# A new order of all operations in a convolution, layer norm and feed-forward kernel, and a scaling in two one-column operations

## The chip, the cores and the metric

The kernel runs on one core of one Trainium2 chip. The metric is the device time of one execution in microseconds (us). A core has a matrix engine (TensorE, PE in the profile, its weight loads PEld), VectorE (DVE), ScalarE (ACT), GpSimd (POOL) and SyncE (SP), which here only issues transfers. Each works through a queue of its own in order and waits for the others by semaphores.

## What is computed

The input `x` has 8 sequences of 4224 tokens with 192 features. Every token first becomes a weighted sum of itself and its six predecessors (a dynamic convolution: 7 weights for each token and each of 8 heads, by a softmax), then goes through a layer norm with gain `g_ln`, a two-layer feed-forward network with 768 hidden features, and a residual addition:

```python
w = np.exp(weight_gen - max); w = w / (np.sum(w, axis=-1, keepdims=True) + 1e-09)
out = np.einsum('bshk,bskhg->bshg', w, x_unf)            # x_unf: the token and 6 predecessors
mu, var = mean and variance of each token's 192 features
xn = (x - mu) / np.sqrt(var + 1e-06) * g_ln
ch = np.maximum(xn @ w_ch1, 0.0) @ w_ch2
return (x + ch).astype(np.float32)
```

(In the last three lines `x` is the convolution's result.) The weights of the network come as 64-bit floats.

## The kernel before

**Tiling.** The 33,792 tokens lie over 128 partitions, 264 columns each. Columns go in parts of 4, 8 or 12 (`PARTS`), the convolution in chunks of up to 6 columns, the network in 66 groups of 4 columns. `x` is kept in a ring of 36 columns.

**Convolution (`conv`).** SyncE loads `x` and the softmax weights `w`. `softmax` makes the exponent's argument with maxima `mx` and sums `sm` on VectorE (L461, L477), operand steps on GpSimd (L463, L481) and exponentials and a logarithm on ScalarE. `conv` multiplies on VectorE (L530): product 0 goes into the buffer `y`, six more, two at a time, into three buffers `pr`. From the fourth chunk on four of the six are added to `y` by GpSimd (L533, steps `a0` to `a3`); the other two are first added to a neighbour in `pr` by a DMA that GpSimd issues and that adds at its destination (L536, steps `d0` and `d1`; here called a sum by DMA).

**Layer norm (`norm`).** ScalarE sums and squares each token (L604, L609), VectorE refines the reciprocal root, ScalarE scales to `xh` (L653). The first two groups are transposed by TensorE (L676), the rest split into a high half (ScalarE, `hl`, L722) and a remainder (GpSimd, `hl`, L724) and transposed by a DMA from SyncE (L728, step `turn`) to `xT`.

**Network.** TensorE multiplies a group in three units (L746, step `unit`) into two PSUM tiles `ph`; of each unit ScalarE writes `hh` (L762) and VectorE the remainder `hlo` (L764), which frees the tile. The second layer runs in two halves a group (L798, steps `p0` and `p1`), the last group in four whole outputs (L827). VectorE adds the result to `y` (L850) and SyncE stores it (L858, step `u`).

**Weights (`weights`).** At the start the 64-bit weights are converted (`from_double`, L916 to L933). `w_scale` sums their squares with TensorE (L944, into `po`) and takes the reciprocal of a power of two from it in four one-column steps on VectorE (L948 to L952); after them it multiplies the gain `g`, two columns, by that number into `gi` (L954). ScalarE scales the weights with `gi`; TensorE makes the low halves (L994, for the second matrix the corrections L1040 and L1041), ScalarE copies them (L999, L1045).

**What sets the order.** Every operation is given to `Plan.op` with a name, and takes the next number from that name's row in the table `PLACE` (L38 on). `Plan.order` sorts all operations by these numbers; each engine's queue is that order, cut to its own operations. It also hands out buffers in this order, each operation to the one that was last used earliest. Two kinds of transfers are kept apart: a transpose waits until the last sum by DMA ahead of it has landed, and the other way round.

```python
o.key, o.place = want, PLACE[want[0]][i]
...
out = sorted(self.ops, key=lambda o: o.place)
...
if o.kind in last:
    o.behind, last[o.kind] = last["turn" if o.kind == "add" else "add"], o
```

Of the kernel before, what the change touches and what calls it, by code (L numbers as in the profile page):

```python
# [38 lines left out]
    'wload': (0, 1, 13, 40, 43, 97, 228, 492, 500, 297, 610, 771, 667, 953, 949, 1143, 1284, 1244, 1047, 1445,  # L39
        1553, 1626, 1733,),  # L40
    'load': (2, 3, 5, 7, 9, 23, 48, 51, 50, 138, 140, 136, 277, 226, 273, 288, 291, 417, 336, 488, 613, 564,
        665, 740, 634, 732, 856, 840, 873, 945, 927, 1011, 1069, 1247, 1287, 1311, 1210, 1378, 1371, 1411, 1492,
        1653, 1517, 1623, 1777, 1703, 1852, 1924, 1915, 1959, 2014, 1954,),
    'w_load': (27, 15, 21,),
    'w_gain': (30, 46, 38,),
    'w_load2': (32,),
    'w_as': (71,),
    'w_av': (80, 83, 86,),
    'w_an': (89,),
    'w_cs': (57,),  # L50
# [12 lines left out]
    'w_d2': (168,),
    'w_h2': (175, 173, 193,),
    'w_l2': (187, 181, 196,),
    'w_lc2': (192, 188, 203,),
    'max': (4, 11, 52, 111, 114, 323, 268, 540, 596, 592, 705, 826, 893, 1097, 1129, 1175, 1347, 1345, 1483,
        1606, 1622, 1723, 1911,),
    'sub': (6, 16, 60, 115, 238, 347, 462, 581, 606, 702, 776, 902, 999, 1102, 1136, 1265, 1369, 1421, 1543,
        1630, 1768, 1814, 2007,),  # L70
    'exp': (8, 22, 66, 147, 263, 364, 491, 601, 636, 744, 803, 931, 1037, 1113, 1144, 1277, 1387, 1449, 1563,
        1638, 1792, 1849, 2041,),
    'sum': (10, 26, 93, 180, 285, 390, 496, 605, 645, 756, 818, 946, 1044, 1138, 1150, 1280, 1436, 1451, 1609,
        1654, 1807, 1890, 2063,),
    'log': (12, 29, 100, 184, 293, 407, 501, 609, 663, 772, 841, 968, 1058, 1147, 1216, 1285, 1450, 1490, 1679,
        1750, 1847, 1894, 2075,),
    'less': (14, 31, 109, 185, 316, 410, 514, 612, 689, 787, 883, 980, 1063, 1166, 1295, 1359, 1456, 1546, 1690,
        1781, 1861, 1935, 2103,),
    'expw': (17, 20, 35, 45, 119, 137, 155, 202, 210, 274, 331, 337, 378, 429, 450, 521, 530, 629, 643, 718,
        731, 811, 830, 904, 936, 1000, 1031, 1116, 1109, 1204, 1215, 1312, 1351, 1415, 1391, 1516, 1500, 1601,  # L80
        1627, 1710, 1726, 1811, 1805, 1871, 1968, 1964, 2039, 2132, 2122, 2206,),
    'keep': (18, 39, 63,),
# [16 lines left out]
    'copy': (54, 73, 101,),  # L99
    'sums': (58, 75, 104, 107, 152, 169, 204, 217, 239, 237, 259, 279, 329, 319, 348, 344, 393, 413, 424, 426,  # L100
# [7 lines left out]
    'squares': (69, 79, 124, 110, 163, 171, 212, 224, 242, 286, 267, 282, 339, 332, 350, 355, 409, 415, 435,  # L108
# [7 lines left out]
    'rstd': (81, 134, 178, 233, 289, 359, 441, 512, 594, 699, 808, 901, 1007, 1110, 1213, 1304, 1426, 1519,  # L116
# [167 lines left out]
def kernel(  # L284
# [673 lines left out]
    def weights():  # L958
        F2 = F // 2
        wac, w2r = Buf("hlo"), Buf("hlo")  # L960
        wa, wc = (wac, "a"), (wac, "c")
        s1, s2, r1, r2, g, gi = (W[k] for k in ("s1", "s2", "r1", "r2", "g", "gi"))
# [69 lines left out]
        z2 = [Buf("ph"), Buf("ph")]  # L1032
# [77 lines left out]
```

## Time and profile before

| | us |
|---|---|
| three timed runs | 860.5, 862.37, 863.0 |
| their median | 862.37 |
| the profiled execution | 856.82 |
| its span, from the first to the last instruction | 855.0 |
| busy in it: TensorE | 820.9 |
| VectorE | 740.9 |
| ScalarE | 691.1 |
| GpSimd | 701.9 |

The profile is of one execution. A timeline row gives the start in us from the span's start, how long it took, the engine, the line of the kernel, the operation, what it writes and reads, and how many equal ones it merges; in brackets stands how long the engine had been idle and what released it. "issue" as the releaser means that the engine waited for nothing that the profile shows. A `q` behind an engine (SPq) marks its sequencer, which issues transfers. "To landing" is the time from a transfer's issue until all of it has arrived.

### The profile page before, as it was taken

The numbers are of one execution on the slowest core, as the hardware profiler recorded it, in microseconds if no ns is written. First come the engines' busy times: TensorE is split into PE (matmuls) and PEld (weight loads), VectorE is DVE, ScalarE is ACT, GpSimd is POOL, SyncE is SP. The second block draws the span as 40 slices with busy tenths as digits, with TensorE's granted clock in tenths as the row PEclk, the third lists the DMA queues.
The fourth block names the chain that finished last, engine by engine and source line by source line (L and its number), as shares of the span: only waits on it lengthen the run. The fifth ranks groups of instructions, "written<-read, shape, count | busy, mean of one in ns | idle before, by whom it ended". The sixth has DMA issues, their size and how long they took to land.

```text
span 855.0 us, 37401 instructions
## 1 busy us (share of the span) xinstructions
PE 820.9 (96%) x16696; PEld 804.3 (94%) x16696; DVE 740.9 (87%) x692; ACT 691.1 (81%) x1804; POOL 701.9 (82%) x402
## 2 busy tenths in 40 slices
PE   6669999999999999999999999999999999999997
PEld 5349999999999999999999999999999999999997
DVE  7999999999999999999999899889898797655442
ACT  5889988889988889989987888798878987786431
POOL 4799999999999999999999889997898678572200
PEclk9789999999999999999999999999999999999999
DMA  8689999889998999978989599897786853555332
GB/s 238 152 169 181 211 168 186 187 185 214 175 212 153 195 214 175 197 166 193 209 163 228 133 169 196 148 192 165 160 201 150 164 127 80 110 114 86 67 105 57
DMA packets 133888, 140.89 MB, mean 165 GB/s; under 512 B 104294, under 2 KB 106222, under 8 KB 133726
## 3 DMA queue, kind: packets, MB, share of 16 engines
q1 hardware_dynamic: 120190, 88.16, 47.8%
q0 software_dynamic: 13536, 50.34, 30.6%
q8 instruction: 130, 2.13, 1.0%
q14 instruction: 32, 0.26, 0.1%
HBM read 36.43 MB, written 25.95 MB: 73 GB/s over the span
## 4 chain that ended last, share of the span: by engine, by line
PE 88%; DVE 6%; ACT 3%; issue 2%; DMA 1%; SPq 0%; DVEq 0%; ACTq 0%
PE po L798 44%; PE ph L746 43%; DVE pr L530 3%; DVE hlo L764 1%; PE ph L827 1%; DMA x<-in_x_dram 1%; ACT xh L653 1%; DVE y L530 1%; ACT junk L604 0%; ACT junk L609 0%; PE ph L1040 0%; DVE mx L461 0%; DVE hlo L930 0%; ACT hh L762 0%; SPq L423 0%
## 5 line engine op out<-in xcount | busy, mean ns | idle before, releaser
L533 POOL TENSOR_TENSOR y<-y,pr 128x1152 f32<-128x1152 f32 (+1 forms) x188 | 482.4, 2583 | 25.6 <-DVE y L530 8.9
L746 PE MATMUL ph<-xT,c_w 64*128 64x256 f16 x7128 | 416.5, 269 | 3.0 <-DVE hlo L764 2.2
L746 PEld LDWEIGHTS <-c_w 64*128 64x128 f16 x7128 | 386.9, 94 | 9.4 <-issue 7.1
L798 PE MATMUL po<-c_w2l,hh 64*128 64x192 f16 x3120 | 392.1, 243 | 2.5 <-issue 2.5
L798 PE MATMUL po<-c_w2h,hlo 64*128 64x192 f16 x3120 | 392.0, 243 | 1.7 <-issue 1.7
L798 PE MATMUL po<-c_w2h,hh 64*128 64x192 f16 x3120 | 391.8, 243 | 0.1
L798 PEld LDWEIGHTS <-hh 64*128 64x128 f16 x6240 | 340.2, 94 | 4.1 <-issue 3.9
L530 DVE TENSOR_TENSOR pr<-x,wn 128x2304 f32<-128x2304 f32 (+2 forms) x147 | 333.2, 2276 | 4.3 <-POOL y L533 2.7
L764 DVE SCALAR_TENSOR_TENSOR hlo<-ph,hh 128x1024 f16<-128x1024 f32 x198 | 238.7, 1217 | 81.4 <-ACT hh L762 81.0
L762 ACT ACTIVATE hh<-ph 128x1024 f16<-128x1024 f32 x198 | 200.2, 1014 | 88.8 <-PE ph L746 81.9
L798 PEld LDWEIGHTS <-hlo 64*128 64x128 f16 x3120 | 213.6, 94 | 2.3 <-issue 2.3
L724 POOL TENSOR_TENSOR hl<-xh,hl 128x768 f16<-128x768 f32 x64 | 115.7, 1857 | 41.3 <-ACT hl L722 41.2
L653 ACT ACTIVATE xh<-y,s 128x192 f32<-128x192 f32 x264 | 126.4, 538 | 11.5 <-DVE s L641 7.2
L609 ACT ACTIVATE junk<-y,s 128x192 f32<-128x192 f32 x264 | 120.0, 455 | 9.5 <-PE po L798 3.2
L536 POOL DMA_DIRECT2D pr<-pr x94 | 93.3, 1083 | 38.1 <-DVE pr L530 14.3
L604 ACT ACTIVATE junk<-y 128x192 f32<-128x192 f32 x264 | 95.4, 361 | 12.3 <-PE po L798 5.2
L850 DVE SCALAR_TENSOR_TENSOR y<-po,c_fs,y 128x768 f32<-128x768 f32 (+1 forms) x83 | 68.2, 835 | 7.4 <-PE po L798 7.3
L530 DVE TENSOR_TENSOR y<-x,wn 128x1152 f32<-128x1152 f32 (+2 forms) x50 | 59.9, 1199 | 0.0
L722 ACT ACTIVATE hl<-xh 128x768 f16<-128x768 f32 x64 | 53.6, 838 | 2.6 <-PE po L798 1.7
L604 ACT ACTIVATION_READ_ACCUMULATOR junk<-y 128x1 f32 x264 | 50.0, 189 | 0.0
L609 ACT ACTIVATION_READ_ACCUMULATOR junk<-y,s 128x1 f32 x264 | 49.8, 189 | 0.0
L463 POOL TENSOR_TENSOR e<-w,mx 128x672 f32<-128x672 f32 (+2 forms) x23 | 34.6, 1503 | 5.0 <-issue 2.8
(79 smaller groups left out, 302.5 us busy)
## 6 DMA issues: line engine op xcount, KB each, us to landing
pr<-pr POOLq DMA_DIRECT2D x68, 576.0 KB, 6.8
x<-in_x_dram SPq DMA_DIRECT2D x34, 576.0 KB, 6.5
out_dram<-y SPq DMA_DIRECT2D x34, 576.0 KB, 5.5
pr<-pr POOLq DMA_DIRECT2D x26, 384.0 KB, 5.1
w<-in_weight_gen_dram SPq DMA_DIRECT2D x21, 336.0 KB, 6.2
x<-in_x_dram SPq DMA_DIRECT2D x14, 384.0 KB, 6.1
out_dram<-y SPq DMA_DIRECT2D x13, 384.0 KB, 3.7
x<-in_moe_w_ch_dram SPq DMA_DIRECT2D x1, 1152.0 KB, 12.2
```

The costliest lines, as they stand in the source:

```text
L530: E.tensor_tensor(out=ov, in0=xv, in1=wv, op=ALU.mult)
L533: Q.tensor_tensor(out=flat(0), in0=flat(0), in1=flat(k), op=ALU.add)
L536: return Q.dma_start(flat(to), flat(k), accum_op=ALU.add, max_dma_last_dim=CHUNK * D * 4)
L604: A.activation(junk, at(y)[:, j, :], AF.Identity, scale=-SQ / D, accum_out=at(s4)[:, 3, t : t + 1])
L609: A.activation(junk, at(y)[:, j, :], AF.Square, scale=SQ, bias=at(s4)[:, 3, t : t + 1], accum_out=at(s4)[:, 0, t : t + 1])
L653: A.activation(paired(xh, t), at(y)[:, i, :].rearrange("p (c q) -> p c q", q=P // 2), AF.Identity, bias=at(s4)[:, 3, g + t : g + t + 1], s ...
L724: lambda xh=xh, hl=hl: Q.tensor_tensor(out=halves(hl, True), in0=pairs(xh), in1=halves(hl, False), op=ALU.subtract),
L746: T_.matmul(ph[:, r, v * 2 * P : (v + 1) * 2 * P], W["w1"][rows, WB[r][c], w, f : f + P], xv[rows, a, c, :, :], start=(v == 0 and k == 0), ...
L762: lambda: A.activation(at(hh)[:, us, :], at(ph), AF.Relu), [ph], [(hh, u)])
L764: lambda: V.scalar_tensor_tensor(out=at(hlo)[:, us, :], in0=at(ph), scalar=0.0, in1=at(hh)[:, us, :], op0=ALU.max, op1=ALU.subtract),
L798: made.append(T_.matmul(at(po)[:, z, e * D : (e + 1) * D], token(b, 2 * z + e, j)[rows], W[w][rows, j, :], start=(ph == 0 and e == 0 and k ...
L850: V.scalar_tensor_tensor(out=ysl, in0=at(po)[:, zs[0] : zs[-1] + 1, : 2 * D], scalar=W["fs"][:, 0:1], in1=ysl, op0=ALU.mult, op1=ALU.add)
```

## The change

The table `PLACE` gets other numbers in nearly every row, found by a search in which the transfers' model also holds TensorE's instruction packets. The names, their counts and what each operation computes stay. In the sequence of TensorE the units, halves and outputs of the network keep their order among each other; transfers, VectorE, ScalarE and GpSimd work in another order, and through it some buffers change hands. Beside it the gain is scaled column by column. Of the table two rows stand for all:

```diff
-    'w_gain': (30, 46, 38,),
+    'w_gain': (44, 30, 42,),
...
-    'hop': (252, 299, 338, 377, 419, 455, 490, 527, 562, 593, 635, 674, 706, 747, 780, 820, 854, 885, 920, 957,
+    'hop': (256, 301, 337, 382, 421, 457, 491, 529, 561, 595, 634, 671, 705, 741, 778, 815, 850, 884, 921, 954,
...
-        w_scale("s1", s1[:, 0:2], 128.0, r1, [(wa, "sq"), (wc, "sq")], "r1", [(gi, g)], ["g0", "g1t", "g1b"], ["gi"])
+        w_scale("s1", s1[:, 0:2], 128.0, r1, [(wa, "sq"), (wc, "sq")], "r1", [(gi[:, i : i + 1], g[:, i : i + 1]) for i in range(2)],
+                ["g0", "g1t", "g1b"], ["gi"])
```

VectorE at the scaling of the gain, before and then after (`mx` are softmax maxima, `c_r` the scale, `c_gi` the scaled gain, `pr` a product of the convolution):

```order
L930 SCALAR_TENSOR_TENSOR hlo1_91<-x_63,po0_106 128x384
L461 TENSOR_REDUCE mx1_93<-w0_64 128x96
L461 TENSOR_REDUCE mx0_92<-w1_65 128x96
L948 TENSOR_SCALAR c_r1_125<-po0_106 128x1
L949 TENSOR_SCALAR c_r1_125<-c_r1_125 128x1
L951 TENSOR_SCALAR c_r1_125<-c_r1_125 128x1
L952 RECIPROCAL c_r1_125<-c_r1_125 128x1
L954 TENSOR_SCALAR c_gi_122<-c_g_121,c_r1_125 128x2
L530 TENSOR_TENSOR pr3_79<-x_63,wn0_102 128x2x768
```

```order
L930 SCALAR_TENSOR_TENSOR hlo1_91<-x_63,po0_106 128x384
L461 TENSOR_REDUCE mx1_93<-w0_64 128x96
L948 TENSOR_SCALAR c_r1_125<-po0_106 128x1
L949 TENSOR_SCALAR c_r1_125<-c_r1_125 128x1
L951 TENSOR_SCALAR c_r1_125<-c_r1_125 128x1
L952 RECIPROCAL c_r1_125<-c_r1_125 128x1
L954 TENSOR_SCALAR c_gi_122<-c_g_121,c_r1_125 128x1 x2
L461 TENSOR_REDUCE mx0_92<-w1_65 128x96
L530 TENSOR_TENSOR pr0_76<-x_63,wn0_102 128x2x768
```

One of the two maxima moved from ahead of the scale to behind it, and the gain takes two operations.

GpSimd at four sums by DMA (L536) near the middle of the program, before and then after (`y` with `pr` are additions of the convolution, `e` softmax steps, `hl` splits ahead of a transpose):

```order
L533 TENSOR_TENSOR y3_70<-y3_70,pr1_77 128x1152
L536 DMA pr4_80<-pr4_80 128x1152
L536 DMA pr2_78<-pr2_78 128x1152
L463 TENSOR_TENSOR e1_97<-w2_66,mx0_92 128x672
L536 DMA pr3_79<-pr3_79 128x1152
L536 DMA pr1_77<-pr1_77 128x1152
L533 TENSOR_TENSOR y5_72<-y5_72,pr0_76 128x1152 x2
```

```order
L536 DMA pr2_78<-pr2_78 128x1152
L533 TENSOR_TENSOR y7_74<-y7_74,pr4_80 128x1152
L536 DMA pr3_79<-pr3_79 128x1152
L463 TENSOR_TENSOR e1_97<-w1_65,mx0_92 128x672
L536 DMA pr0_76<-pr0_76 128x1152
L533 TENSOR_TENSOR y7_74<-y7_74,pr4_80 128x1152
L533 TENSOR_TENSOR y7_74<-y7_74,pr2_78 128x1152
L533 TENSOR_TENSOR y7_74<-y7_74,pr3_79 128x1152
L724 TENSOR_TENSOR hl1_84<-xh1_82,hl1_84 128x2x384
L724 TENSOR_TENSOR hl0_83<-xh0_81,hl0_83 128x2x384
L533 TENSOR_TENSOR y3_70<-y3_70,pr4_80 128x1152 x2
L481 TENSOR_TENSOR e0_96<-e0_96,sm0_94 128x672
```

Three of the four moved apart by one operation each, and the fourth went behind the last row shown.

GpSimd ahead of the transposes of the columns 24 to 27 and 28 to 31, before and then after (the splits are `hl0` and `hl1`):

```order
L533 TENSOR_TENSOR y1_68<-y1_68,pr0_76 128x768
L724 TENSOR_TENSOR hl0_83<-xh1_82,hl0_83 128x2x384
L536 DMA pr3_79<-pr3_79 128x768
L533 TENSOR_TENSOR y1_68<-y1_68,pr1_77 128x768
L536 DMA pr0_76<-pr0_76 128x768
L724 TENSOR_TENSOR hl1_84<-xh0_81,hl1_84 128x2x384
```

```order
L533 TENSOR_TENSOR y1_68<-y1_68,pr2_78 128x768
L536 DMA pr0_76<-pr0_76 128x768
L533 TENSOR_TENSOR y1_68<-y1_68,pr1_77 128x768
L536 DMA pr2_78<-pr2_78 128x768
L724 TENSOR_TENSOR hl0_83<-xh1_82,hl0_83 128x2x384
L533 TENSOR_TENSOR y0_67<-y0_67,pr4_80 128x768
L533 TENSOR_TENSOR y0_67<-y0_67,pr3_79 128x768
L724 TENSOR_TENSOR hl1_84<-xh0_81,hl1_84 128x2x384
```

The first split moved behind both sums, the second also behind two additions.

## Rows read from the trace of the kernel before

**Rows 1.** The page: busy time, share, instructions by engine; packets, MB, share of q8.

```profile
PE 820.9 (96%) x16696; PEld 804.3 (94%) x16696; DVE 740.9 (87%) x692; ACT 691.1 (81%) x1804; POOL 701.9 (82%) x402
...
q8 instruction: 130, 2.13, 1.0%
```

**Rows 2.** Busy time in one stretch: length, busy (instructions), clock, DMA share, GB/s.

```profile
58.45:850.55 792.10, 784.84 (x16561) 778.20 (x16560) 688.67 (x614) 650.15 (x1685) 661.21 (x367) 1.00 0.80 164
```

**Rows 3.** Waits of PE after 58.5 us: us in total, times, longest.

```profile
PE po L798 <- issue: 4.2, 6, 1.4
PE ph L746 <- DVE hlo L764: 2.2, 4, 0.9
...
PE ph L746 <- issue: 0.6, 1, 0.6
```

**Rows 4.** Timeline of PE at its longest such wait.

```profile
473.39 0.25 PE L798 MATMUL po<-c_w2l,hh 64*128 64x192 f16 x1 [1.38 <-issue]
```

**Rows 5.** Timeline of POOL ahead of that wait: the sums by DMA.

```profile
455.17 1.77 POOL L536 DMA_DIRECT2D pr<-pr  x2 [0.55 <-DMA xT<-hl]
...
457.63 2.46 POOL L536 DMA_DIRECT2D pr<-pr  x2
```

**Rows 6.** Line L536 from 457 to 460 us: durations (ns), starts, landing.

```profile
L536 POOL DMA_DIRECT2D pr<-pr x2: 1402/1479/1556, 457.6 to 458.7; - x2
...
DMA to landing us min/median/max: 11.8/13.3/14.7
```

**Rows 7.** Line L536 over the whole span: landing.

```profile
DMA to landing us min/median/max: 3.9/6.4/14.7
```

**Rows 8.** Timeline of all engines from 32.2 to 37 us.

```profile
32.36 1.60 DVE L461 TENSOR_REDUCE mx<-w 128x96 f32<-128x672 f32 x2
...
33.88 0.15 DVE L948 TENSOR_SCALAR c_r<-po 128x1 f32<-128x1 f32 x1
...
34.44 0.16 DVE L952 RECIPROCAL c_r<-c_r 128x1 f32<-128x1 f32 x1
34.60 1.81 POOL L533 TENSOR_TENSOR y<-y,pr 128x768 f32<-128x768 f32 x1
...
34.63 1.80 DVE L954 TENSOR_SCALAR c_gi<-c_g,c_r 128x2 f32<-128x2 f32 x1
...
36.35 1.74 DVE L530 TENSOR_TENSOR pr<-x,wn 128x1536 f32<-128x1536 f32 x1
```

**Rows 9.** Timeline of all engines from 58 to 64.2 us.

```profile
58.20 0.32 PE L1041 MATMUL ph<-c_w2h,minus 128*128 128x384 f16 x1 [1.69 <-ACT c_w2h L1036]
...
58.45 4.30 PE L746 MATMUL ph<-xT,c_w 64*128 64x256 f16 x72
...
61.30 1.00 ACT L762 ACTIVATE hh<-ph 128x1024 f16<-128x1024 f32 x1
...
62.34 1.23 DVE L764 SCALAR_TENSOR_TENSOR hlo<-ph,hh 128x1024 f16<-128x1024 f32 x1 [1.74 <-ACT hh L762]
...
63.61 0.83 PE L746 MATMUL ph<-xT,c_w 64*128 64x256 f16 x12 [0.86 <-DVE hlo L764]
```

**Rows 10.** Timeline of all engines from 111 to 121 us.

```profile
111.15 1.65 POOL L724 TENSOR_TENSOR hl<-xh,hl 128x768 f16<-128x768 f32 x1
...
115.11 1.17 POOL L536 DMA_DIRECT2D pr<-pr  x1
...
120.18 1.41 SPq L728 DMA_TRANSPOSE xT<-hl  x1
```

**Rows 11.** Line L728 from 120 to 121 us: landing.

```profile
DMA to landing us min/median/max: 5.8/5.8/5.8
```

**Rows 12.** Timeline of PE from 126.4 us: the first two units of that group.

```profile
126.88 4.17 PE L746 MATMUL ph<-xT,c_w 64*128 64x256 f16 x72
```

**Rows 13.** Waits of POOL at sums by DMA: us in total, times, longest.

```profile
POOL pr L536 <- DVE pr L530: 14.3, 8, 4.3
POOL pr L536 <- DVE hlo L764: 10.2, 1, 10.2
```

More of the change, by code (lines that the diff above doesn't have):

```diff
@@ L65 @@
[L65 to L81, printed above, removed]
@@ L82 @@
-    'keep': (18, 39, 63,),
[16 rows of a table removed]
-    'copy': (54, 73, 101,),
-    'sums': (58, 75, 104, 107, 152, 169, 204, 217, 239, 237, 259, 279, 329, 319, 348, 344, 393, 413, 424, 426,
[7 rows of a table removed]
-    'squares': (69, 79, 124, 110, 163, 171, 212, 224, 242, 286, 267, 282, 339, 332, 350, 355, 409, 415, 435,
[7 rows of a table removed]
-    'rstd': (81, 134, 178, 233, 289, 359, 441, 512, 594, 699, 808, 901, 1007, 1110, 1213, 1304, 1426, 1519,
-        1619, 1722, 1822, 1934, 2029, 2108, 2217, 2281, 2346,),
-    'newton': (87, 146, 182, 245, 294, 366, 445, 515, 600, 703, 810, 905, 1010, 1115, 1218, 1313, 1431, 1522,
[10 rows of a table removed]
@@ L129 @@
-    'thi': (139, 179,),
-    'tlo': (177, 186,),
[26 rows of a table removed]
-    'turn': (220, 283, 318, 328, 406, 412, 478, 484, 555, 560, 622, 639, 660, 723, 760, 738, 834, 853, 867, 943,
[3 rows of a table removed]
-    'halo': (229, 431, 753, 1073, 1357, 1621, 2047,),
-    'unit': (200, 207, 215, 223, 231, 246, 264, 271, 292, 311, 317, 334, 352, 358, 375, 391, 397, 414, 428, 437,
[10 rows of a table removed]
-    'relu': (208, 216, 221, 234, 247, 255, 275, 295, 304, 322, 325, 345, 361, 367, 384, 398, 404, 421, 443, 446,
[10 rows of a table removed]
-    'hlo': (211, 219, 227, 240, 262, 258, 287, 303, 309, 326, 342, 354, 369, 383, 394, 418, 408, 425, 448, 459,
[14 rows of a table removed]
@@ L199 @@
-    'hop': (252, 299, 338, 377, 419, 455, 490, 527, 562, 593, 635, 674, 706, 747, 780, 820, 854, 885, 920, 957,
[15 rows of a table removed]
+    'wload': (0, 1, 13, 46, 27, 89, 233, 501, 418, 293, 663, 767, 843, 1040, 619, 1151, 1288, 1188, 957, 1444,
+        1521, 1620, 1736,),
+    'load': (2, 3, 5, 7, 9, 22, 48, 97, 93, 163, 154, 161, 86, 332, 231, 214, 295, 420, 341, 490, 503, 666, 575,
+        632, 650, 725, 857, 821, 926, 948, 924, 1007, 1072, 1246, 1242, 1309, 1211, 1371, 1359, 1473, 1482,
+        1625, 1547, 1598, 1675, 1755, 1859, 1838, 1820, 1986, 2009, 1955,),
@@ new lines @@
+    'w_load': (38, 15, 20,),
+    'w_gain': (44, 30, 42,),
+    'w_load2': (32,),
+    'w_as': (83,),
+    'w_av': (91, 94, 99,),
+    'w_an': (104,),
+    'w_cs': (49,),
+    'w_cv': (61, 63, 64,),
+    'w_cn': (92,),
+    'w_s1': (116, 118,),
+    'w_d': (132, 125,),
+    'w_h': (130, 124,),
+    'w_l': (135, 128,),
+    'w_lc': (150, 133,),
+    'w_m': (167, 158, 136, 140,),
+    'w_c2s': (90, 100, 139,),
+    'w_c2v': (101, 105, 106, 108, 111, 113, 146, 149, 151,),
+    'w_c2n': (143, 119, 153,),
@@ new lines @@
+    'w_s2': (157, 164, 228,),
+    'w_d2': (170,),
+    'w_h2': (184, 171, 183,),
+    'w_l2': (189, 186, 197,),
+    'w_lc2': (192, 193, 202,),
+    'max': (4, 11, 56, 120, 115, 300, 290, 565, 601, 543, 775, 887, 913, 1079, 1102, 1217, 1326, 1231, 1436,
+        1508, 1685, 1776, 1966,),
+    'sub': (6, 16, 62, 123, 199, 363, 454, 571, 605, 685, 785, 893, 978, 1097, 1130, 1267, 1406, 1421, 1519,
+        1604, 1765, 1817, 2013,),
+    'exp': (8, 21, 67, 173, 246, 373, 476, 598, 643, 715, 801, 909, 1029, 1111, 1154, 1282, 1418, 1465, 1587,
+        1651, 1828, 1855, 2029,),
@@ new lines @@
+    'sum': (10, 26, 72, 178, 255, 393, 498, 607, 651, 727, 840, 952, 1038, 1144, 1184, 1285, 1441, 1517, 1611,
+        1682, 1841, 1866, 2040,),
+    'log': (12, 29, 77, 181, 299, 411, 505, 610, 664, 771, 864, 975, 1042, 1166, 1257, 1347, 1464, 1530, 1614,
+        1705, 1862, 1875, 2066,),
+    'less': (14, 31, 84, 191, 309, 425, 514, 612, 697, 777, 889, 993, 1064, 1199, 1263, 1350, 1484, 1565, 1656,
+        1748, 1865, 1943, 2099,),
+    'expw': (17, 25, 36, 58, 112, 145, 156, 206, 241, 263, 319, 361, 379, 438, 448, 522, 546, 629, 662, 709,
+        728, 789, 826, 916, 966, 1002, 1023, 1086, 1117, 1216, 1209, 1286, 1365, 1378, 1408, 1509, 1500, 1600,
+        1570, 1684, 1727, 1781, 1802, 1894, 1950, 1978, 2064, 2151, 2108, 2110,),
@@ new lines @@
+    'keep': (18, 40, 39,),
[16 rows of a table added]
+    'copy': (53, 70, 107,),
+    'sums': (55, 71, 109, 114, 126, 147, 203, 211, 227, 266, 264, 273, 324, 329, 349, 342, 402, 388, 414, 428,
[7 rows of a table added]
+    'squares': (59, 73, 121, 117, 175, 165, 236, 220, 232, 284, 271, 276, 334, 338, 351, 354, 409, 417, 426,
[7 rows of a table added]
+    'rstd': (78, 134, 176, 245, 289, 357, 434, 508, 591, 699, 808, 901, 1008, 1108, 1207, 1313, 1426, 1507,
+        1629, 1719, 1823, 1932, 2024, 2125, 2220, 2286, 2344,),
+    'newton': (85, 142, 185, 247, 292, 364, 440, 513, 597, 702, 810, 907, 1009, 1112, 1210, 1315, 1439, 1516,
[10 rows of a table added]
@@ new lines @@
+    'thi': (141, 187,),
+    'tlo': (180, 194,),
[26 rows of a table added]
+    'turn': (224, 287, 321, 328, 405, 413, 480, 484, 553, 559, 622, 645, 658, 733, 761, 746, 831, 854, 868, 945,
[3 rows of a table added]
+    'halo': (218, 569, 774, 1136, 1351, 1644, 2067,),
+    'unit': (201, 207, 217, 226, 235, 249, 269, 275, 294, 311, 318, 336, 353, 358, 375, 392, 397, 415, 431, 437,
[10 rows of a table added]
+    'relu': (209, 215, 223, 238, 242, 261, 279, 291, 303, 322, 331, 345, 362, 367, 384, 400, 406, 424, 441, 456,
[10 rows of a table added]
+    'hlo': (213, 221, 229, 244, 265, 268, 286, 297, 308, 330, 340, 352, 368, 376, 386, 403, 423, 427, 450, 462,
[14 rows of a table added]
```

24 lines of the change are left out of this document (removed), and 236 rows, old and new, of the table PLACE.

## Prediction

> **What bounds the kernel now.** I read the page first, then TensorE's waits, then the stretches where it waits. TensorE is busy 96% of the span [rows 1], and from its first product of the network at 58.45 to its last at 850.55 for 784.84 of 792.10 us, at a granted clock of 1.00 [rows 2]. That busy time the change cannot touch: in the order of instructions TensorE's units, halves and last outputs stand in the same sequence in both kernels. It can touch the 58.45 us ahead of them and the 7.26 us of idle time within.
>
> TensorE's waits after 58.5 us tell what the 7.26 are [rows 3]: 2.2 us in four waits for VectorE's `hlo`, and 4.2 + 0.6 = 4.8 us in seven waits whose releaser is "issue", that is, nothing that the profile shows. The longest, 1.38 us, ends at 473.39 inside a half output [rows 4], where no operand can be late any more. What can be late is TensorE's own code. The page lists a queue of instruction packets beside the two data queues, 130 packets with 2.13 MB, as a share of the same 16 engines, and TensorE has 2 x 16,696 products and weight loads against 692 + 1804 + 402 instructions of the other three [rows 1]: nearly all of that code is its own. Ahead of the wait at 473.39 four sums by DMA were issued within 3.5 us, two from 455.17 and two from 457.63 [rows 5]. The later two, issued at 457.6 and 458.7, took 11.8 and 14.7 us to land [rows 6], against a median of 6.4 over all 94 [rows 7]; the last so landed at 473.4, as the wait ended. So I read it thus: a bunch of transfers holds up the code, and TensorE runs dry. This is inferred from the coincidence; no row names a late packet as the releaser.
>
> **The change, part by part.** *Scaling of g_ln.* Before, `c_gi` is one operation on two columns. It starts at 34.63, 0.03 us after an addition of GpSimd (34.60, 1.81 us), ends 0.02 us behind it (1.80 us), and VectorE's next operation starts at 36.35 [rows 8]. A step on one column takes 0.19 us from start to start (34.44 to 34.63) [rows 8]. Two of them cost 0.38 instead of 1.72: 1.34 us less on VectorE, if it was the second column that made the operation long. The Trainium skill ("SBUF — State Buffer", Who interferes with whom) says that a VectorE operation in a two-port mode and a GpSimd operation exclude each other for a whole instruction, whichever starts second waiting for the other's end. The common end of the two rows agrees, and by that rule the term is the 1.34. Without it a step on one column might wait just as long, and the term would be 0.
>
> *Order around it.* VectorE is full in this stretch, so what stands ahead counts. Before, two reductions `mx` (32.36 to 33.88, so 0.76 each [rows 8]) lie over the time in which TensorE adds up the squares that the scale needs. After, one of them stands ahead and the other behind the scale. The scale can't start sooner, so 0.76 us stay uncovered, and the moved reduction costs its 0.76 afterwards. VectorE's gain is 1.34 - 0.76 = 0.58 us.
>
> *First product.* It does not profit at once. The first unit starts at 58.45, after the third correction of w2, which had waited 1.69 us for ScalarE [rows 9]. After, another 0.76 us reduction moves ahead of what the corrections wait for on VectorE, so they begin 0.76 - 0.58 = 0.18 us later; and the third one shares a PSUM tile with the first two and waits for their evacuation, no longer for ScalarE's scaled weights. I take these as even: 58.45. What comes free is behind it. Units 0 and 1 take 4.30 us, so unit 0 ends at 60.6, but ScalarE came to its `hh` only at 61.30; VectorE stood idle for 1.74 us until 62.34, and TensorE began unit 2 at 63.61 [rows 9]. After the change fewer operations stand on ScalarE between the corrections and `hh`, and it can start at 60.75: 0.55 us. Bounds: 1.34 us if all of the saving comes through; 0 if ScalarE is as late as before.
>
> *The table of places.* It moves the other engines' operations and the transfers. The sums by DMA stand less close: of the 94, three fall within four successive rows of GpSimd's order 15 times before and 6 times after. Of the bunch of four, three stay, with an addition between the first and the second and a softmax step between the second and the third, and the fourth goes behind eight further rows. I let the waits for code shrink as the bunches do: 4.8 x (15 - 6) / 15 = 2.9 us. Bounds: all 4.8 go; or none go, and new bunches give as much again (+4.8). I keep the middle because the longest of the seven waits stands behind the bunch that is taken apart. The `hlo` waits (2.2 us) I leave, and the tail has the same order in both.
>
> **Sum.** The profiled execution took 856.82 us, 855.0 of it span; the change makes it 856.82 - 0.55 - 2.9 = 853.4. The median of the timed runs is 862.37, 5.55 above the profiled one. I carry these 5.55 over unchanged: 862.37 - 3.45 = 858.9 us (-0.4%).
>
> **Rivals.** *Only the start gains (861.8).* The waits for code move instead of going, since there are as many transfers and bytes as before. For it: seven waits in 792 us are few, and may fall elsewhere. Against it: the slowest landing of all sums (14.7 us [rows 7]) belongs to the bunch that is taken apart. 862.37 - 0.55 = 861.8. The Trainium skill ("Runtime: NRT & Kernel Launch", Instruction fetch mechanics) says that code streams in blocks of 16 KiB while the engine runs, and that crossing a block is mostly hidden; by that rule the table has nothing to win here and this rival is right. The "issue" of [rows 3] speaks against it.
>
> *GpSimd's queue blocks ahead of a transpose (slower).* Its place is the group of columns 24 to 27, the tightest that I found. Before, the last sum ahead of its transpose is issued at 115.11; the transpose, which waits for that landing, at 120.18 [rows 10]; it takes 5.8 us [rows 11] and lands at 126.0, and the unit starts at 126.88 [rows 12]: 0.9 us to spare. Before, GpSimd's split `hl` of this group stands ahead of the last two sums, after the change behind both. So the last sum is issued one split, 1.65 us [rows 10], sooner; but both splits now queue behind a DMA issue that waits for VectorE's product. If it waits w, TensorE loses w - 1.65 - 0.9, and nothing gives that back. Such waits lasted up to 4.3 us for a product and once 10.2 for an `hlo` [rows 13]: a loss of 1.75 to 7.65 us, and with no gain in code 863.6 to 869.5. The kernel is slower by over 0.3% from w = 5.7 us on. Against it: VectorE is earlier by 0.58 us here, not later. That the change doesn't do what it says is excluded for the order, which the rows show; for the scale it is the 0 above.
>
> **How the numbers follow.** 0.3% is 2.6 us, about what a measurement of this kernel can tell from no change: faster is below 859.8, slower above 865.0. Chances: the forecast 0.56, of which 0.05 ends within 0.3% because fewer waits go; only the start 0.32, with 0.01 of it faster; the blocked queue 0.12, with 0.02 within 0.3%. So faster 0.52, same 0.38, slower 0.10. The range: at the low end the start gives 1.34, all 4.8 us of code go, and so do 2.2 of the 5.55 us that only the timed runs show: 854.0. At the high end the start gives nothing and the queue blocks for the 4.3 us seen: 864.1. One in ten lies beyond each.
>
> **What would show it.** In the profile after: `c_gi` twice at about 0.15 us; the first unit between 58.2 and 58.7 and unit 2 near 63.1; "issue" ahead of TensorE's products at about 2 us; no sum that takes over 12 us to land; no wait of TensorE for `xT`. I am wrong if "issue" stays at 4 us or more (the first rival), if TensorE waits for a landing of `xT` between 100 and 240 us (the second), or if the time falls below 854: then the timed runs lose more to late code than the profiled one shows.

## The result and the profile after

The changed kernel takes 850.65 us, the median of 6 runs (848.64 to 852.42), beside 862.68 for the kernel before (857.66 to 864.97, 6 runs): a ratio of the means of 0.9863, 95% interval 0.9830 to 0.9896. On another occasion (15) it was 0.9869 (0.9836 to 0.9902). The forecast was 858.9, with a range from 854.0 to 864.1. So the sign was right, and the gain, 12.0 us, is over three times the 3.5 that were forecast.

The profiled execution took 848.79 us, 847.0 of it span. TensorE's row, the queue of code packets, and TensorE's busy time from its first product of the network to the end of its last (columns as in [rows 1, 2]):

```profile
PE 819.0 (97%) x16696; PEld 767.3 (91%) x16696; DVE 740.1 (87%) x693; ACT 690.3 (81%) x1804; POOL 702.1 (83%) x402
...
q8 instruction: 130, 2.13, 1.1%
```

```profile
57.88:842.47 784.59, 782.61 (x16561) 741.69 (x16560) 688.96 (x614) 648.70 (x1683) 660.18 (x366) 1.00 0.80 164
```

The network takes 784.59 instead of 792.10 us [rows 2], and starts 0.57 us earlier. There are as many code packets as before. What has gone are most of TensorE's waits after 58 us, here as us in total, times, longest (before: [rows 3]):

```profile
PE ph L746 <- DVE hlo L764: 1.6, 3, 0.7
PE po L798 <- issue: 0.2, 1, 0.2
```

"issue" fell from 4.8 us in seven waits to 0.2 in one. The slowest sum by DMA now takes 10.8 us to land instead of 14.7 [rows 7]:

```profile
DMA to landing us min/median/max: 3.8/5.8/10.8
```

At the scaling of the gain, VectorE's and GpSimd's timelines (start, length; before: [rows 8]):

```profile
27.40 5.63 POOL L533 TENSOR_TENSOR y<-y,pr 128x768 f32<-128x768 f32 x3
35.82 1.37 POOL L463 TENSOR_TENSOR e<-w,mx 128x672 f32<-128x672 f32 x1 [2.80 <-DVE mx L461]
```

```profile
34.34 0.33 DVE L954 TENSOR_SCALAR c_gi<-c_g,c_r 128x1 f32<-128x1 f32 x2
34.89 0.85 DVE L461 TENSOR_REDUCE mx<-w 128x96 f32<-128x672 f32 x1 [0.21 <-issue]
```

Two operations take 0.33 us where one took 1.80. But GpSimd stands idle beside them, from 33.0 to 35.8; before, it was adding. The first units of the network (before: [rows 9]):

```profile
57.88 4.10 PE L746 MATMUL ph<-xT,c_w 64*128 64x256 f16 x72
62.39 2.14 PE L746 MATMUL ph<-xT,c_w 64*128 64x256 f16 x36 [0.41 <-DVE hlo L764]
```

```profile
60.06 1.02 ACT L762 ACTIVATE hh<-ph 128x1024 f16<-128x1024 f32 x1
```

ScalarE comes to `hh` at 60.06 instead of 61.30, and unit 2 starts at 62.39 instead of 63.61.

**Lost time, counted from start to start.** Products follow each other every 0.082 us when nothing is late. A wait's idle time in the profile begins only where the product ahead is modelled to end, some 0.25 us after its start, so it hides a part of each wait. The product at 473.39 of [rows 4] shows 1.38 us idle, but starts 1.62 us after the product ahead of it: 1.54 us are lost. Counted this way for every gap of more than 0.16 us, with the packet in mind that ended just ahead of it (below), the network divides thus:

| us, from the first product's start to the last's | before | after |
|---|---|---|
| lost behind late code (waits) | 6.63 (10) | 0.89 (3) |
| lost behind VectorE's `hlo` | 3.10 (5) | 2.29 (4) |
| other gaps | 0.40 | 0.09 |
| the rest | 781.7 | 781.1 |
| sum | 791.8 | 784.35 |

The rest is nearly the same: in all fifteen experiments it lies between 780.8 and 784.0, and the four above 783 (1, 6, 11 and 14) had stretches at half the clock within the network. So of the 8.03 us between the two profiled executions, 5.7 are code, 0.8 `hlo`, 0.6 the start, 0.3 other gaps and 0.6 the rest.

### The profile page after: what moved, and what is told of

It is laid out like the page before. It is cut to its first block, busy times and chain, and to the rows that moved or that the text cites. A ratio compares the mean times of both kernels' runs of the same rounds, so it can differ in the third digit from the quotient of the medians.

```text
span 847.0 us, 37402 instructions
## 1 busy us (share of the span) xinstructions
PE 819.0 (97%) x16696; PEld 767.3 (91%) x16696; DVE 740.1 (87%) x693; ACT 690.3 (81%) x1804; POOL 702.1 (83%) x402
## 4 chain that ended last, share of the span: by engine, by line
PE 91%; DVE 5%; issue 1%; ACT 1%; DVEq 0%
PE po L798 45%; PE ph L746 45%; DVE pr L530 2%; PE ph L827 1%; PE ph L1041 0%; DVE y L530 0%; ACT hh L762 0%; DVE hlo L764 0%; DVE hlo L930 0%; DVE sm L477 0%; DVE mx L461 0%; DVE ph L927 0%; DVE ph L925 0%; DVE po L927 0%; DVE po L925 0%
## 5 line engine op out<-in xcount | busy, mean ns | idle before, releaser
L746 PE MATMUL ph<-xT,c_w 64*128 64x256 f16 x7128 | 411.0, 269 | 1.7 <-DVE hlo L764 1.6
L798 PE MATMUL po<-c_w2h,hlo 64*128 64x192 f16 x3120 | 383.7, 243 | 0.2 <-issue 0.2
L798 PE MATMUL po<-c_w2h,hh 64*128 64x192 f16 x3120 | 383.7, 243 | 0.1
L798 PE MATMUL po<-c_w2l,hh 64*128 64x192 f16 x3120 | 383.7, 243 | 0.0
L746 PEld LDWEIGHTS <-c_w 64*128 64x128 f16 x7128 | 347.8, 94 | 39.4 <-issue 3.1
L764 DVE SCALAR_TENSOR_TENSOR hlo<-ph,hh 128x1024 f16<-128x1024 f32 x198 | 239.9, 1220 | 74.6 <-ACT hh L762 74.1
L798 PEld LDWEIGHTS <-hh 64*128 64x128 f16 x6240 | 284.3, 94 | 3.2 <-issue 0.4
L798 PEld LDWEIGHTS <-hlo 64*128 64x128 f16 x3120 | 153.6, 94 | 0.4 <-issue 0.4
L536 POOL DMA_DIRECT2D pr<-pr x94 | 94.0, 1063 | 27.5 <-DVE pr L530 22.4
L604 ACT ACTIVATE junk<-y 128x192 f32<-128x192 f32 x264 | 95.1, 360 | 11.2 <-PE po L798 4.5
L481 POOL TENSOR_TENSOR e<-e,sm 128x672 f32<-128x672 f32 (+2 forms) x23 | 36.7, 1595 | 6.4 <-ACT sm L479 6.4
```

The costliest lines, as they stand in the source:

```text
L536: return Q.dma_start(flat(to), flat(k), accum_op=ALU.add, max_dma_last_dim=CHUNK * D * 4)
L604: A.activation(junk, at(y)[:, j, :], AF.Identity, scale=-SQ / D, accum_out=at(s4)[:, 3, t : t + 1])
L746: T_.matmul(ph[:, r, v * 2 * P : (v + 1) * 2 * P], W["w1"][rows, WB[r][c], w, f : f + P], xv[rows, a, c, :, :], start=(v == 0 and k == 0), ...
L764: lambda: V.scalar_tensor_tensor(out=at(hlo)[:, us, :], in0=at(ph), scalar=0.0, in1=at(hh)[:, us, :], op0=ALU.max, op1=ALU.subtract),
L798: made.append(T_.matmul(at(po)[:, z, e * D : (e + 1) * D], token(b, 2 * z + e, j)[rows], W[w][rows, j, :], start=(ph == 0 and e == 0 and k ...
```

## Is it code? The packets in the trace

The prediction inferred late code from a coincidence. The packets can be seen. The kernel before, its DMA queues (packets, MB, share of 16 engines) in two stretches ahead of the wait that ends at 473.39, 464.75 to 471.05 and 471.0 to 472.1:

```profile
q0 software_dynamic: 224, 0.92, 80.3%
q1 hardware_dynamic: 108, 0.47, 23.3%
```

```profile
q1 hardware_dynamic: 96, 0.27, 67.7%
q0 software_dynamic: 10, 0.01, 6.7%
q8 instruction: 1, 0.02, 5.2%
```

For 6.3 us the two data queues fill the engines' time (80 and 23%) and no code comes; then one packet passes, from 471.12 to 472.04, and 1.35 us behind its end TensorE goes on. So it is each time: all ten waits counted above as code end 1.25 to 1.50 us behind the end of a packet, and the three of the changed kernel 1.21 to 1.36.

How late a packet is can be told too. 33,392 products and weight loads over 130 packets are 257 a packet. I take 256, and as a packet's delay the time from the start of TensorE's instruction number 256 x j to the start of packet j. From the fifth packet on, the smallest delay is 3.6 us. In the kernel before the median is 5.3 and the largest 9.9; in the changed one 5.0 and 8.3. The ten waits of before follow the ten packets with a delay over 8.1 us, the three of after the three such packets.

And what makes a packet late is the number of data transfers in flight, of any kind. For 1,080 packets of nine kernels that move all of their data (both kernels, a repeat of before, and six of the experiments below), by the number of loads, stores, transposes and sums that were issued and not yet landed 3.6 us after instruction 256 x j:

| in flight | 0 | 1 | 2 | 3 | 4 | 5 |
|---|---|---|---|---|---|---|
| packets | 90 | 348 | 438 | 155 | 47 | 2 |
| mean delay, us | 4.3 | 4.9 | 5.7 | 6.5 | 7.9 | 10.3 |
| delay over 8.1 us | 0 | 7 | 10 | 24 | 22 | 2 |

A straight line through them gives each load 1.0 us, each sum 0.85, each store 0.7 and each transpose 0.6; it explains a third of the spread. In the kernel before, 25 of 120 packets had three or more in flight, in the changed one 14. But 17 of the 65 packets with a delay over 8.1 us had fewer than three, and 156 of the 204 packets with three or more stayed under it. This is a correlation; the experiments have to bear it out.

## The experiments

In kernels whose table is written out anew, lines from L435 on stand 20 higher: L766, L784 and L818 are L746, L764 and L798. "Lost" is counted as above, in the profiled execution.

**1. The scaling alone.** Only the edit of the scaling, in the old order.

```diff
-        ..., [(gi, g)], ["g0", "g1t", "g1b"], ["gi"])
+        ..., [(gi[:, i : i + 1], g[:, i : i + 1]) for i in range(2)], ["g0", "g1t", "g1b"], ["gi"])
```

> The kernel before with one edit: g_ln is scaled in two one-column operations; the table of places is the old one. Theory A (most of the gain is that TensorE's instruction packets come in time, through the order of the transfers): the two operations take 0.15 to 0.2 us each, the first units come up to 1.3 us earlier, the waits of TensorE with the releaser issue stay at 4 to 5 us, and the time is 861.4 to 862.7, within 0.3% of before. Theory B (the gain is the scaling and what follows from it at the start): 851 to 855.

Measured: 863.74 us, ratio 1.0049 (1.0021 to 1.0076): slower, if anything. The two operations did what they should. VectorE and GpSimd:

```profile
35.15 0.33 DVE L974 TENSOR_SCALAR c_gi<-c_g,c_r 128x1 f32<-128x1 f32 x2
```

```profile
35.11 1.83 POOL L553 TENSOR_TENSOR y<-y,pr 128x768 f32<-128x768 f32 x1
```

They run beside GpSimd's addition in 0.33 us, so it was the second column that made the operation last as long as the addition. But late code cost 11.2 us in ten waits, mostly near the places of before. No transfer was moved in the order; everything merely came at slightly other times. TensorE's waits, 9.5 us where theory A expected 4 to 5:

```profile
PE po L818 <- issue: 7.9, 6, 1.9
...
PE ph L766 <- issue: 1.6, 2, 0.9
```

Theory B falls: the scaling carries nothing of the gain. Theory A's time (861.4 to 862.7) was passed as well, on the slow side.

**2. The order alone.** The new order, the gain scaled in one operation.

```diff
-        ..., [(gi[:, i : i + 1], g[:, i : i + 1]) for i in range(2)], ["g0", "g1t", "g1b"], ["gi"])
+        ..., [(gi, g)], ["g0", "g1t", "g1b"], ["gi"])
```

> The changed kernel with one edit undone: g_ln is scaled in one operation on two columns, in the new order. Theory A: the operation takes about 1.8 us if it again ends with an operation of GpSimd, the first units come 0 to 1.3 us later than in the changed kernel, no more than 1 us of waits with the releaser issue, 850.6 to 852. Theory B: 859 to 862.

Measured: 851.07 us, ratio 0.9902 (0.9868 to 0.9936), 0.8 us lost behind late code. The one operation on two columns took no 1.8 us:

```profile
34.98 0.23 DVE L974 TENSOR_SCALAR c_gi<-c_g,c_r 128x2 f32<-128x2 f32 x1
```

```profile
28.04 5.62 POOL L553 TENSOR_TENSOR y<-y,pr 128x768 f32<-128x768 f32 x3
36.04 1.36 POOL L483 TENSOR_TENSOR e<-w,mx 128x672 f32<-128x672 f32 x1 [2.38 <-DVE mx L481]
```

GpSimd is idle from 33.7 to 36.0. In the new order there is nothing to collide with, and the split is superfluous. The operation on two columns took 0.23 us beside an idle GpSimd here and 1.80 beside a busy one [rows 8]; the two on one column took 0.33 together beside a busy one (1). The Trainium skill ("SBUF — State Buffer", SBUF: two separate sides) says that a VectorE operation in a two-port mode and a GpSimd operation exclude each other for a whole instruction. The 0.23 and the 1.80 agree with it; which mode an operation ran in, no run shows.

**3 and 4. Start and rest exchanged.** The first 300 operations, up to TensorE's ninth unit near 76 us, of one table, the others of the other.

```diff
 old_start_new_rest
-    operations 0 to 299 in the order of the new table, split scaling
+    operations 0 to 299 in the order of the old table, one scaling
     all others in the order of the new table
```

> The first 300 operations are those of the old table in their old order (with the scaling in one operation), all others follow in the new order; TensorE is at its ninth unit by then, near 76 us. Theory A: waits with the releaser issue at most 1.5 us, 851 to 853. Theory B: the start of before, so 860 to 862.

```diff
 new_start_old_rest
     operations 0 to 299 in the order of the new table, split scaling
-    all others in the order of the new table
+    all others in the order of the old table
```

> The reverse: the first 300 operations in the new order with the split scaling, all others in the old order. Theory A: first unit near 57.9 us as in the changed kernel, but the waits with the releaser issue stay at 4 us or more, 860 to 862. Theory B: 850 to 853.

Measured: old start and new rest 851.55 us, ratio 0.9920 (0.9890 to 0.9949), 1.7 us lost behind late code; new start and old rest 858.69, ratio 0.9995 (0.9968 to 1.0022), 6.9 lost. TensorE's waits for nothing that shows, after 62 us, of the first and then of the second:

```profile
PE po L818 <- issue: 1.4, 2, 0.8
```

```profile
PE po L818 <- issue: 4.6, 6, 1.2
...
PE ph L766 <- issue: 0.8, 1, 0.8
```

Theory A holds against B: the gain lies behind 76 us, and it goes with the code. But with the new start the first unit came at 59.40 in the second, not near 57.9, and its time lies below the 860 to 862 expected.

**5. Before again.** The kernel before, for a second profiled execution.

> The kernel before, unchanged, for a second profiled execution. Theory A: its waits with the releaser issue are 4 to 8 us and stand at other places too, more of them where the execution takes longer; a wait follows each packet that starts over 8.1 us after TensorE began the 256 instructions of that packet's count. Theory E (the longer timed executions are long for another reason, such as a lower clock at the start): the waits stay at 4.8 us though the execution is longer.

Measured: 860.00 us, ratio 1.0006 (0.9973 to 1.0039); the profiled execution took 859.28 and lost 7.8 us to late code in eight waits, four of them near 454 to 476 us. As theory A says, its eight waits are behind the eight packets with a delay over 8.1 us. Its first product came at 59.1, so the start is a part of the difference, as theory E has it. Executions differ in what they lose, and mostly at the same places.

**6. Sums by DMA moved apart.** The old order, 23 sums moved by an operation or two of GpSimd (here one of the places; SyncE's and GpSimd's operations in order).

```diff
 d0 29
+sub 17
 d1 29
-sub 17
 d1 31
+a0 29
 d0 30
-a0 29
```

> The kernel before with nothing but 23 sums by DMA moved later in the order, each behind the next operation of GpSimd, so that from the 300th operation on no two stand back to back where that is possible: three within four rows of GpSimd's order 6 times instead of 15. Theory A: some waits with the releaser issue go, 1 to 3 us left of 4.8, time 857 to 861. Theory D (it is not the closeness of the sums; loads, stores and transposes matter as much): 4 to 6 us stay, 861 to 864.

Measured: 860.87 us, ratio 0.9998 (0.9972 to 1.0025); 9.7 us lost behind late code. TensorE's waits with the releaser "issue" were 8.4 us, more than theory A (1 to 3) and even D (4 to 6) expected; the time lies at the edge of both. That the closeness of the sums does not decide is right in D, its amount is not. Near 455 us the four sums were now issued from 454.96 to 460.58 instead of 455.17 to 458.68: still four transfers at a time were in flight, first a load, a store and two of the sums, at last all four sums. TensorE's waits from 450 to 480:

```profile
PE po L818 <- issue: 3.9, 3, 2.5
```

By the prediction's measure, how close the sums stand, this kernel is as good as the changed one, and yet it gains nothing.

**7. Sums brought together.** The changed kernel, 38 sums moved to just ahead of the next one (one place shown).

```diff
 sub 16
+a0 29
 d0 29
-a0 29
+sub 17
 d1 29
-sub 17
 d0 30
```

> The changed kernel with nothing but 38 sums by DMA moved later, to just ahead of the next one: three within four rows of GpSimd's order 19 times instead of 7. Theory A: the waits for code come back, at least four with the releaser issue, 2 us or more in all, time 853 to 857. Theory D: at most two more such waits, time 850 to 852.5.

Measured: 858.62 us, slower than the changed kernel by some 8 us (ratio to before 0.9977, 0.9952 to 1.0002). 4.8 us were lost behind late code in six waits, and 3.9 behind transposes, each of which waits for the sums ahead of it:

```profile
PE ph L766 <- DMA xT<-hl: 3.4, 3, 2.3
PE ph L766 <- issue: 2.9, 1, 2.9
```

Theory A holds in its sign and its waits; the time is above its 853 to 857, since the transposes come in. So bunches of sums can make the code late; 6 shows that parting them is not enough.

**8 to 10. Less data, same order.** The old order with the sums cut to 16 numbers a partition, then the stores cut to 16 numbers of each sequence and partition, then both. Most of the sums, or of the output, is left out there.

```diff
-            return Q.dma_start(flat(to), flat(k), accum_op=ALU.add, ...)
+            return Q.dma_start(flat(to)[:, :16], flat(k)[:, :16], accum_op=ALU.add, ...)
```

> The kernel before, in its order, but each sum by DMA moves only the first 16 of its up to 1152 numbers per partition, so most of these sums are left out of the computation; every wait stays. Theory A (packets late behind bunched transfers): without the bytes of these transfers TensorE's code comes in time, waits with the releaser issue fall from 4.8 us to under 0.5, time 849 to 854. Theory C (the packets are late for a reason of their own, such as their place in the program): the waits stay at 4 us or more, 859 to 863.

```diff
-                        tokens(out, t0, n), at(y)[:, i : i + n, :].rearrange("p t d -> p (t d)")),
+                        tokens(out, t0, n)[:, :, :16], at(y)[:, i : i + n, :].rearrange("p t d -> p (t d)")[:, :16]),
```

> The kernel before, in its order, but each store of the output writes only 16 of its up to 1152 numbers per sequence and partition, so most of the output is left unwritten; every wait and every sum by DMA stays. Theory F (a packet of code is late when three or more data transfers of any kind are in flight): the stores' bytes count as much as those of the sums, so the lost time behind late packets falls from 6.5 to 8 us to 3 to 5, time 854 to 858. Theory G (the sums by DMA are what holds up the code): 6 us or more stay, 859 to 862.

> The kernel before, in its order, with both the sums by DMA and the stores cut to 16 numbers, so most of the sums and of the output are left out. Theory F: hardly ever three transfers in flight, under 1.5 us lost behind late packets, time 850 to 853. Theory C (a part is late for a reason of its own): 3 us or more stay, as with the sums cut alone, 854 to 856.

| | us | ratio to before | lost behind late code (waits) |
|---|---|---|---|
| sums cut | 854.68 | 0.9921 (0.9888 to 0.9953) | 3.6 (4) |
| stores cut | 852.94 | 0.9915 (0.9886 to 0.9944) | 3.0 (4) |
| both cut | 851.05 | 0.9887 (0.9844 to 0.9930) | 1.8 (2) |

Theory F holds against G: the stores weigh as much as the sums, and with both cut the loss nearly goes, a little above the 1.5 expected. With the stores cut, the time is below F's 854 to 858. With the sums alone cut, A (under 0.5) misses, and C too. The scatter shrinks with the data: with the stores cut ten executions lie between 852.62 and 853.58 us, with both cut six between 850.49 and 851.36, where those of before beside them go from 854.55 to 866.97. With both cut, what stays is one wait at 97.5 us, behind two loads of `x`, a store and a load of `w` issued from 84.3 to 86.3, and one at 531.6:

```profile
PE po L818 <- issue: 1.2, 1, 1.2
PE ph L766 <- issue: 0.2, 1, 0.2
```

**11 and 12. The transfers' places exchanged.** Behind the 300th operation, all loads, stores, transposes and sums at the places of the other table, between the same units; the three compute engines beside TensorE as they were.

```diff
 new_transfers_old_rest
-    load, wload, u, turn, d0, d1: old places
+    load, wload, u, turn, d0, d1: new places (239 of 243)
     all others: old places
```

> The kernel before; from the 300th operation on all transfers (loads, stores, transposes, sums by DMA) stand between TensorE's units as in the new table, 239 of 243 of them, and VectorE, ScalarE and GpSimd keep the old order. Theory F: what counts is when the transfers run, so most of the lost time goes, 1 to 3 us left, time 852 to 856. Theory H (when a transfer can run is set by the engines that feed it, so the places of the transfers alone do little): 5 us or more left, 857 to 861.

```diff
 old_transfers_new_rest
-    load, wload, u, turn, d0, d1: new places
+    load, wload, u, turn, d0, d1: old places (231 of 243)
     all others: new places
```

> The reverse: the changed kernel with 231 of its 243 transfers behind the 300th operation at their old places between TensorE's units. Theory F: the late packets come back, 4 us or more lost, time 855 to 860. Theory H: 1 to 3 us lost, time 850 to 854.

Both are slower than before: 869.74 us (ratio 1.0103, 1.0052 to 1.0153) and 884.65 (1.0272, 1.0224 to 1.0321). In time neither theory is met, since other waits come in. The first lost 3.3 us behind late code, half of what before loses; the second 6.7, as much as before. TensorE's waits after 62 us, first and second:

```profile
PE ph L766 <- DVE hlo L784: 7.9, 10, 1.7
PE po L818 <- ACTq L828: 4.7, 2, 3.9
```

```profile
PE ph L766 <- DVE hlo L784: 21.8, 8, 8.0
PE po L818 <- issue: 3.5, 3, 2.2
```

By the lost time, F is nearer in both (1 to 3 and 4 or more) than H: the late code goes with the transfers' places, as far as kernels with so many other waits can tell. But transfers that fit one order of the engines hold up another: the table is good only as a whole.

**13. One place thinned out.** The old order with four operations moved near 455 us: `load 39`, a load of `x`; `u 25`, a store; and the last two of the four sums of [rows 5]. SyncE's and GpSimd's operations in order:

```diff
 a3 28
-load 39
-u 25
 d0 29
...
 sub 17
-d1 31
-d0 30
 a0 29
 a1 29
+u 25
 u 26
...
 a2 29
+d0 30
 less 16
...
 lo 34
+load 39
 lo 35
...
 a1 30
+d1 31
 load 40
```

> The kernel before with four operations moved near 455 us, where it lost most: one store goes behind all four sums by DMA, one load behind the next transpose's operands, the third sum behind an addition and the fourth behind the next two transposes. Nothing else is touched. Theory F (three or more transfers of any kind in flight make TensorE's next packet late): the waits between 455 and 480 us, 1.9 us in one profiled execution of before and 4.4 in another, fall below 1 us, all others stay; time 857 to 861, 0.2 to 0.5% faster. Theory I (the lateness there is not from these transfers): 2 us or more stay between 455 and 480.

Measured: 854.10 us, ratio 0.9907 (0.9876 to 0.9938). Before, SyncE's queue there, followed by the four sums of [rows 5]; and then the same stretch of this kernel, SyncE and GpSimd:

```profile
449.34 2.04 SPq L728 DMA_TRANSPOSE xT<-hl  x1
452.35 0.56 SPq L437 DMA_DIRECT2D x<-in_x_dram  x1
452.97 10.83 SPq L858 DMA_DIRECT2D out_dram<-y  x2
```

```profile
447.43 1.91 SPq L748 DMA_TRANSPOSE xT<-hl  x1
449.44 12.59 SPq L878 DMA_DIRECT2D out_dram<-y  x2
462.09 0.59 SPq L463 DMA_DIRECT2D w<-in_weight_gen_dram  x1
462.73 1.86 SPq L457 DMA_DIRECT2D x<-in_x_dram  x1
```

```profile
453.16 1.77 POOL L556 DMA_DIRECT2D pr<-pr  x2 [0.45 <-issue]
...
464.26 0.88 POOL L556 DMA_DIRECT2D pr<-pr  x1
```

Between 452 and 459 us, six transfers were issued before and two now. TensorE's busy time from 450 to 480 (columns as in [rows 2]), before, with the four moves, and in the changed kernel:

```profile
450.00:480.00 30.00, 28.36 (x598) 27.69 (x594) 28.08 (x25) 22.98 (x62) 27.91 (x16) 1.00 0.91 202
```

```profile
450.00:480.00 30.00, 30.00 (x649) 30.00 (x646) 29.54 (x26) 24.64 (x66) 26.93 (x15) 1.00 0.80 167
```

```profile
450.00:480.00 30.00, 30.00 (x652) 28.51 (x648) 29.52 (x25) 27.96 (x78) 27.45 (x16) 1.00 0.90 202
```

598 products became 649. All of TensorE's waits there are gone, as theory F says, and the place that the prediction named was the right one. The loss behind late code over the whole program is 2.8 us in five waits, against 6.6 and 7.8 in the two profiled executions of before, of which 2.1 and 4.5 lay between 450 and 480. So outside of it some went too, where F expected all others to stay. The median gained 8.0 us, more than expected (854.10, not 857 to 861); the profiled execution took 852.00, which is 4.8 and 7.3 us less than the two of before.

**14. Every store twice.** The changed kernel, with the output written two times.

```diff
-                    sp(("u", s), lambda ...: SY.dma_start(...),
+                    sp(("u", s), lambda ...: [SY.dma_start(...) for _ in range(2)],
```

> The changed kernel in its order, but every store of the output is issued twice, so 26 MB more are written; the result is the same. Theory F: more transfers in flight, so the late packets come back, 3 us or more lost behind them where the changed kernel lost 0.9; time 853 to 858. Theory I (only the order counts, not how much is in flight): under 1.5 us, 850 to 852.

Measured: 915.28 us, ratio to before 1.0595 (1.0551 to 1.0640), far beyond the expected 853 to 858. Late code is back, 8.2 us in eight waits, as F says. But most of the time went another way: TensorE waited for VectorE and for transposes,

```profile
PE ph L766 <- DVE hlo L784: 16.1, 12, 4.9
PE ph L766 <- DMA xT<-hl: 11.8, 5, 3.1
```

so this run tells only the sign.

**15. After again.** The changed kernel once more.

> The changed kernel, unchanged, for a second profiled execution on this chip. Theory F: at most 2 us lost behind late packets, and of its executions the fastest and the slowest lie within 6 us, where those of before lie 11 to 13 apart; 849 to 852. Theory I: as wide a scatter as before.

Measured: 850.89 us, ratio 0.9869 (0.9836 to 0.9902), 0.6 us lost behind late code in one wait. Its executions took 848.33 to 851.55, those of before beside it 857.74 to 866.75. Theory F holds: with the late code most of the scatter goes too, 3.2 us where before has 9.0.

## Why the prediction was right and wrong

**Right: what TensorE waits for, and where.** The waits with the releaser "issue" were late code. The bunch near 455 us was the worst place, and taking it apart removes the waits behind it (13). The sign and the price of the two operations (0.33 us for the 0.38 assumed) hold.

**Wrong: how much of the code waits goes.** This is the step that failed: "I let the waits for code shrink as the bunches do: 4.8 x (15 - 6) / 15 = 2.9 us". Both factors were off, and the 6 should be 7: counted as the 15 were, so many times three sums fall within four rows of the changed kernel, which would have made the term 2.6. The loss was not the 4.8 us of idle time but 6.6, since the idle time of a wait leaves out the modelled end of the product ahead of it. And the share that goes was 87%, not 60%, because the count was of the wrong thing. It counted sums alone, in GpSimd's rows. Moved apart from 15 to 6, the sums gained nothing (6); four moves that took a load and a store along brought 3.8 to 5.0 us (13). What late packets go with is how many transfers of any kind are in flight: three or more at 25 packets before, at 14 after. That count is not all of it either: 24 such packets in 6 lost 9.7 us, 25 in 7 lost 4.8. The term measured 5.7 us instead of 2.9. The bound of the term, "all 4.8 go", was passed as well, for the first reason.

**Wrong: the 5.55 us carried over.** The prediction carried the distance from the profiled execution to the median over unchanged. Before, it is 5.9 with the six runs; after, 1.9. So 4.0 of the 12.0 us do not show in the two traces at all. The range allowed 2.2 of it. The last sentence of the prediction named this case: below 854, the timed runs lose more to late code than the profiled one. That is likely, though not shown: just one execution of a run has a trace, and the clock at the start differs too (last section). For it speak the runs with less data in flight, where the old order scatters by 1 us instead of 12 (9 and 10), and the old order's profiled executions, 856.82, 858.66, 859.28, 861.51 and 863.80 us (before, 4, 5, 6 and 1), which lost 6.6, 6.9, 7.8, 9.7 and 11.2 us behind late code.

**The start.** In the two traces unit 2 came 1.22 us earlier, not 0.55, inside the bounds of 0 and 1.34, and the first unit 0.57 earlier where none was expected. But a gain at the start is not shown. In the seven profiled executions with the new start (after, 2, 4, 7, 12, 14, 15) the first unit came between 57.70 and 59.40 us and unit 2 between 62.22 and 65.11; with the old start between 57.64 and 59.76, and 62.79 and 64.91. What the scaling does there is another than the prediction's, too: GpSimd is idle beside it, so the one operation would have taken 0.23 us (2). The new order alone ended the collision, and the split was not needed.

**The waits for `hlo`** were left at their size; in the two traces they fell from 3.1 to 2.3 us lost.

**The rivals.** *Only the start gains* is excluded by 3, where the old start keeps the gain. The Trainium skill ("Runtime: NRT & Kernel Launch", Instruction fetch mechanics) says that crossing a block is mostly hidden. That holds for 120 of 130 packets before and for 127 after; the other ten of before cost 6.6 us. *GpSimd's queue blocks a transpose* did not happen: no wait for `xT` in the changed kernel. That transposes can come late, 7 shows with 3.9 us; by way of the splits in GpSimd's queue, it does not show.

## What to carry to other kernels

Where TensorE's products are tens of thousands of instructions, their code is a stream of transfers on the same engines as the data. Waits with no releaser behind long products are to be set beside the packets of the code queue: if each ends just behind a packet, thin out the places where three or more transfers of any kind are in flight, whichever queues issue them. Count lost time from start to start of the products, not by idle time. Such a count finds the places; how much each will give it does not tell, so try a move of few operations, as 13 does. And one execution's distance to the median is no constant: where the loss hangs on coincidences, the scatter goes with it.

## What the runs showed of the hardware

**The code's margin.** In both kernels a packet of 16 KB that starts up to 8.1 us behind its instruction costs nothing, and one that starts later stops TensorE until 1.2 to 1.5 us behind the packet's end. In the other kernels the bound is less sharp: some packets over 8.1 us cost nothing, and a few from 7.7 us on stop it. Each transfer in flight goes with 0.6 to 1.0 us more of a packet's delay, whether it comes from SyncE or from GpSimd.

**Late code can cost clock, too.** In 1 the granted clock was 0.50 (1.2 GHz) from 477.73 to 481.14 us, just behind the longest wait for code (2.08 us, until 477.33). TensorE ran 40 products there, and 68 in as long a stretch behind as long a wait in 5, at 1.00 (2.4 GHz). In 6 it was the same from 476.15 to 479.57. The "lost" of 1 and 6 leaves that out; it stands in their rest, 783.1 and 783.3 us instead of 781.7.

**Small shifts and places far off.** The split alone (1) moved no transfer in the order, and late code cost 11.2 us instead of 6.6 to 7.8; the median was 863.74, beside 859.14 for before. Perhaps small shifts at 35 us change which transfers meet at 470. One trace does not show it, where executions of before alone differ by 13 us.

**The clock at the start.** The granted clock of TensorE ahead of the network differs between executions. In 2 (order alone), busy for 12.06 of 18 us and waiting in between, TensorE was held at 0.50 (1.2 GHz) up to 62 us; in the changed kernel, busy for 11.64 of them, it had 1.00 (2.4 GHz) from 58 on. From 40 us, first 2, then the changed kernel:

```profile
40.00:58.00 18.00, 12.06 (x31) 7.27 (x32) 17.38 (x29) 15.37 (x43) 17.11 (x13) 0.50 0.89 191
58.00:60.00 2.00, 2.00 (x13) 0.77 (x13) 2.00 (x2) 1.65 (x5) 2.00 (x3) 0.50 0.79 128
```

```profile
40.00:58.00 18.00, 11.64 (x37) 6.91 (x36) 17.38 (x28) 15.13 (x42) 17.33 (x13) 0.57 0.90 192
58.00:60.00 2.00, 2.00 (x40) 1.79 (x38) 1.92 (x2) 1.97 (x7) 2.00 (x3) 1.00 0.74 108
```

The first 72 products took 5.55 us there and 4.10 here. In whole executions it goes with up to 3 us: of the six in 15, the two with a mean clock of 0.991 and 0.992 took 848.3 and 848.8 us, the four with 0.983 or 0.984 took 850.7 to 851.6. Why the clock rises later in some executions of one kernel, no run here shows.
